# Attention from each row's eight largest scores, with values fetched by index, in front of two dense layers

## The chip, the core and the metric

The kernel runs on one core of one Trainium2 chip. The core has TensorE (PE in the profile; PEld is its weight loads), VectorE (DVE), ScalarE (ACT), GpSimd (POOL) and SyncE (SP), which here only issues transfers. The metric is the device time of one execution in microseconds (us); the median of three runs is given.

## The reference

Attention with a threshold, and then two dense layers (token blocks B=4, H=8 heads, S=576 rows, D=64; 2304 tokens, 512 wide, 2048 hidden). The inputs `q`, `k`, `v` and `moe_w_in` are drawn normal and multiplied by 8 over what stands here; `tau` is 0.02. The dense weights lie in memory as 64-bit numbers.

```
scores = scale * np.matmul(q, k.transpose(0, 1, 3, 2))
thresh = np.max(scores, axis=-1, keepdims=True) - tau
scores = np.where(scores >= thresh, scores, -1000000000.0)
attn = np.exp(scores - max) ; attn = attn / (sum + 1e-09)
x = (attn @ v), heads side by side            # 2304 x 512
h = x @ w_in ; y = (s * relu(h)**2 + b) @ w_out               # layer one
h = y @ w_in2 ; out = (max(h, 0) + alpha * min(h, 0)) @ w_out2   # layer two
```

Only the scores within 0.02 of a row's largest take part. With the reference's inputs that is one to seven of a row's 576 scores; no row has eight.

## The kernel before, in words

**Attention.** 16 pairs of heads (4 blocks of 4 pairs) give 9 tiles each of 128 rows by 576 scores, 144 tiles in all. A tile is scored in two halves of 288 columns into a two-bank PSUM buffer `sc` (L859); there are two such buffers. DVE takes the row's largest from it (L869), POOL works out the threshold (L871), ACT takes the exponential (L873), DVE multiplies it by the mask and sums (L875). The kept exponentials `e` are turned on PE by products with identity matrices (`flip`, L400 and L402), split into a high and a low part (`gh`, `gl`: L1032 and L1047 on POOL, L1035 on ACT, L1037 on DVE) and multiplied by the values `vt` (L979). The result, divided by the sums, goes to a buffer `xs` in memory, already turned.

**Layer one, in two passes.** Products are three matmuls each (`mm3`, L608 to L610: low by high, high by low, high by high). Ten of the 16 pairs of hidden tiles (`NA`) of the first 1536 tokens are worked during attention, in the gaps that it leaves PE, and their part of the output goes to memory (`ya`). The other six, and all 16 for the last two blocks of 384 tokens, come after attention, with `ya` added back.

**Layer two** multiplies its matrices by seven block products in place of eight (`seven`, L551; sums of blocks are made on DVE and POOL at L573 and L586), also with `mm3`.

**Weights** are made from the 64-bit words on DVE (L496 to L505: three or four passes over 128x512) and ACT, one set per 128x512 words.

**What sets the order.** A planner (`Plan`, L217) takes tasks with a cost, an engine or several, buffers and a rank, and writes out one fixed instruction order for every engine. `MOVES`, a table of some 100 lines, shifts the ranks of single tasks by their number:

```
        ways = [(engine, us, n if rank is None else rank)] if isinstance(engine, str) else engine
        t.ways = [(e, u, (r + MOVES.get(n, 0), n)) for e, u, r in ways]
```

On an engine nothing overtakes: an instruction that waits holds up all that stand behind it.

## Time and profile before

| | us |
|---|---|
| runs | 1098.36, 1092.99, 1094.26; median 1094.26 |
| span of the profiled execution | 1091.7 |
| PE, DVE, ACT, POOL busy in it | 1065.7, 886.6, 730.2, 344.3 |

The span is what the profiler saw from the first to the last instruction; it lies 2.6 us below the median of the runs. Busy time counts matmuls, weight loads, and work on data, not the issuing of transfers. An engine that is busy nearly all of the span sets the time if its work comes one after the other.

### The profile page before, as it was taken

The page shows a single profiled execution, that of the slowest core. Times are in us where ns is not written, and L with a number is a line of the kernel's source. Part 1 is how long each engine was busy: PE and PEld are TensorE (multiplying, and loading weights), DVE is VectorE, ACT ScalarE, POOL GpSimd, SP SyncE. Part 2 cuts the span into 40 slices and gives each one's busy share as a digit, 9 for nine tenths or more (in the row PEclk, how much of TensorE's full clock was granted, in tenths as well). Part 3 has the DMA queues.
Part 4 walks back from the last instruction along what each step waited for, and adds up shares of the span by engine and source line. Part 5 has one row for each costly group of instructions (what it writes and reads, how often), then busy time and mean ns, then how long its engine had stood idle before and what let it go on. Part 6 is the DMA issues. An engine that isn't in the chain of part 4 may idle for free.

```text
span 1091.7 us, 21462 instructions
## 1 busy us (share of the span) xinstructions
PE 1065.7 (98%) x7074; PEld 1015.3 (93%) x7074; DVE 886.6 (81%) x2005; ACT 730.2 (67%) x1737; POOL 344.3 (32%) x475
## 2 busy tenths in 40 slices
PE   8999999999999999999999999999999999999998
PEld 7767889989999989999999999999999999999998
DVE  5989888978888788837766695588889999999872
ACT  5899877867887778734443364477768997565551
POOL 1567754754564366520000020110103341112100
PEclk9999999999999999999999999999999999999999
DMA  6655475476555653425375766248586464554531
GB/s 150 188 168 155 111 162 144 109 181 152 128 128 142 150 114 95 113 80 188 116 248 181 240 214 212 73 142 259 196 262 228 162 208 147 152 155 130 155 84 39
DMA packets 195182, 170.89 MB, mean 157 GB/s; under 512 B 73216, under 2 KB 173568, under 8 KB 195072
## 3 DMA queue, kind: packets, MB, share of 16 engines
q1 hardware_dynamic: 192112, 167.31, 53.9%
q10 hardware_dynamic: 2960, 2.23, 0.8%
q8 instruction: 55, 0.90, 0.4%
q14 instruction: 55, 0.45, 0.1%
HBM read 98.97 MB, written 49.28 MB: 136 GB/s over the span
## 4 chain that ended last, share of the span: by engine, by line
PE 78%; DVE 6%; ACT 6%; DMA 5%; issue 2%; SPq 1%; POOL 1%; DVEq 0%; ACTq 0%; POOLq 0%
PE bank L608 12%; PE bank L609 11%; PE bank L610 11%; PE bank_b L608 8%; PE bank_b L609 8%; PE bank_b L610 8%; PE sc L859 7%; PE bank L979 6%; DMA q<-hq 4%; PE bank L402 3%; PE bank L400 3%; ACT e L873 1%; DMA gf<-yat 1%; DVE e L875 1%; DMA stg<-in_moe_w_out_dram 1%
## 5 line engine op out<-in xcount | busy, mean ns | idle before, releaser
L875 DVE SCALAR_TENSOR_TENSOR e<-sc,mx,e 128x576 f32<-128x576 f32 x144 | 116.3, 811 | 14.0 <-ACT e L873 10.5
L869 DVE TENSOR_REDUCE mx<-sc 128x1 f32<-128x576 f32 x144 | 107.4, 750 | 20.9 <-PE sc L859 20.0
L873 ACT ACTIVATE e<-sc,mx 128x576 f32<-128x576 f32 x144 | 107.0, 747 | 10.9 <-DVE mx L869 10.2
L402 PE MATMUL bank<-eyes_r,e 128*128 128x128 f32 (+1 forms) x320 | 88.8, 287 | 0.0
L608 PE MATMUL bank<-xt,wa 128*128 128x480 f32 (+3 forms) x221 | 81.4, 368 | 1.0 <-ACT rest L639 0.7
L871 POOL TENSOR_SCALAR mx<-mx,tau_s 128x1 f32<-128x1 f32 x144 | 47.4, 330 | 91.0 <-DVE mx L869 76.9
L609 PE MATMUL bank<-xt,wa 128*128 128x480 f32 (+3 forms) x221 | 74.5, 337 | 0.0
L610 PE MATMUL bank<-xt,wa 128*128 128x480 f32 (+3 forms) x221 | 74.3, 336 | 0.0
L608 PE MATMUL bank<-gt,wa 128*128 128x384 f32 (+4 forms) x209 | 73.4, 351 | 0.1
L610 PE MATMUL bank<-gt,wa 128*128 128x384 f32 (+4 forms) x209 | 69.7, 333 | 0.0
L609 PE MATMUL bank<-gt,wa 128*128 128x384 f32 (+4 forms) x209 | 69.6, 333 | 0.0
L979 PE MATMUL bank<-gl,vt 128*128 128x256 f32 (+1 forms) x192 | 63.8, 334 | 0.0
L979 PE MATMUL bank<-gh,vt 128*128 128x256 f32 (+1 forms) x192 | 57.7, 302 | 0.0
L1035 ACT ACTIVATE gh<-bank 128x256 fp32r<-128x256 f32 (+1 forms) x96 | 39.5, 411 | 23.8 <-PE bank L402 19.0
L1037 DVE TENSOR_TENSOR gl<-bank,gh 128x256 fp32r<-128x256 f32 (+1 forms) x96 | 43.4, 452 | 12.4 <-ACT gh L1035 11.4
L1047 POOL TENSOR_TENSOR gr<-gf,gh 64x256 fp32r<-64x256 f32 (+1 forms) x48 | 39.4, 820 | 42.9 <-DVE gl L1045 38.6
L402 PEld LDWEIGHTS bank<-eyes_r,e 128*128 128x128 f32 (+1 forms) x320 | 44.5, 139 | 4.2 <-DVE e L875 0.2
L1032 POOL TENSOR_TENSOR gl<-gf,gh 128x256 fp32r<-128x256 f32 (+1 forms) x48 | 38.6, 805 | 22.7 <-ACT gh L1030 12.7
L502 DVE SCALAR_TENSOR_TENSOR n<-stg,n 128x512 int32<-128x512 int32 x64 | 44.7, 699 | 1.0
L608 PEld LDWEIGHTS bank<-xt,wa 128*128 128x128 f32 x221 | 42.4, 192 | 3.3 <-ACT rest L639 1.1
L859 PE MATMUL sc<-k,q 128*128 128x288 f32 x184 | 41.3, 349 | 3.9 <-DMA q<-hq 2.7
L660 ACT ACTIVATE gt<-rest 128x384 fp32r<-128x384 f32 x56 | 29.2, 524 | 23.0 <-DVE rest L658 22.2
(710 smaller groups left out, 4192.6 us busy)
## 6 DMA issues: line engine op xcount, KB each, us to landing
stg<-in_moe_w_in_dram SPq DMA_DIRECT2D x32, 512.0 KB, 3.9
stg<-in_moe_w_out_dram SPq DMA_DIRECT2D x32, 512.0 KB, 3.7
gf<-gw SPq DMA_DIRECT2D x41, 192.0 KB, 2.4
gw<-gf SPq DMA_DIRECT2D x56, 128.0 KB, 2.8
q<-hq SPq DMA_DIRECT2D x24, 256.0 KB, 5.4
qo<-hq SPq DMA_DIRECT2D x24, 256.0 KB, 5.2
xt<-xs SPq DMA_DIRECT2D x14, 384.0 KB, 4.3
yf<-yb SPq DMA_DIRECT2D x24, 192.0 KB, 2.8
```

Of the source, the lines that this page charges most:

```text
L402: nc.tensor.transpose(to, part(x), one)
L502: add("DVE", dve(DM), lambda: nc.vector.scalar_tensor_tensor(ni(), word(0), 29, ni(), op0=ALU.logical_shift_right, op1=ALU.bitwise_or), (n ...
L608: nc.tensor.matmul(o, lhsT=wl, rhs=mh, start=first, stop=False, skip_group_check=on_top)
L609: nc.tensor.matmul(o, lhsT=wh, rhs=ml, start=False, stop=False, skip_group_check=on_top)
L610: nc.tensor.matmul(o, lhsT=wh, rhs=mh, start=False, stop=last, skip_group_check=on_top)
L859: nc.tensor.matmul(sp.t[:, x, :HS], lhsT=o[0][:, c], rhs=o[1][:, x * HS:(x + 1) * HS], start=n == 0, stop=n == len(passes) - 1)
L869: add("DVE", dve(S), lambda sp=sp, mx=mx: nc.vector.tensor_reduce(mx.t[:, 0:1], sp.t[:, :, :HS], op=ALU.max, axis=AX.XY, negate=True), (sp ...
L871: t2 = add("POOL", 0.26, lambda mx=mx: nc.gpsimd.tensor_scalar(mx.t[:, 1:2], mx.t[:, 0:1], -1.0, tau_s, op0=ALU.mult, op1=ALU.subtract), ( ...
L873: add("ACT", act(S, 1), lambda sp=sp, mx=mx, e=e: nc.scalar.activation(halves(e.t), sp.t[:, :, :HS], AF.Exp, bias=mx.t[:, 0:1]), (sp, mx), ...
L875: add("DVE", dve(S) + 0.065, lambda sp=sp, mx=mx, e=e, col=col, sums=sums: nc.vector.scalar_tensor_tensor(halves(e.t), sp.t[:, :, :HS], mx ...
L979: nc.tensor.matmul(o.t[:, :n], lhsT=w.rearrange("p a b -> p (a b)"), rhs=m.t[:, :n], start=c == first and x == 0, stop=c == last and x == ...
L1037: add("DVE", dve(n), lambda hi=hi, lo=lo, gt=gt: nc.vector.tensor_tensor(lo.t[:, :n], gt.t[:, :n], f32(hi.t[:, :n]), op=ALU.subtract), (gt ...
```

## The change

- **Scores to SBUF.** Each half of the scores goes to its own PSUM bank, and ACT copies it to a buffer `sc` of 128x576 in SBUF (two such buffers). The exponential, mask and sum over 576 columns go, and so do the turns of `e`, its splits and the products with the values.
- **`top`.** DVE takes the eight largest of a row and their places (`nc.vector.max`, `nc.vector.max_index`, L648 and L649). All that follows works on these eight: `places` L666, `masks` L673 to L675, exponential L678, `shares` L681 to L685, `codes` L690 to L694, once for a pair's 9 tiles (4 or 5 in the first block).
- **`fetch`.** For the two largest of every row POOL issues an indirect transfer that fetches 128 rows of 64 values by index (L518), 2 per tile, 288 in all. They are multiplied by their shares and added (L707, L712) and stored to a buffer `zn` in memory.
- **`rest`.** The third to seventh of a row, where the threshold keeps them, are collected once for a unit of 16 or 36 tiles (five units): the largest eight codes of every partition, 4 or 5 of them fetched (23 fetches in all) and added in memory by indirect transfers that add (L763, 23 of them, each waiting for the one before).
- **`alarm` and `dense`.** Flags are raised where an eighth score is kept, two places of one row tie, or a unit has more entries in a partition than it fetches. At the end every engine reads the flags (`values_load`, L1158) and branches (L1159); where one is raised, `dense` works everything out again in a plain way. With the reference's inputs none is raised.
- **Layer one in one pass.** All 16 pairs of hidden tiles are held in SBUF, and seven `BLOCKS` of tokens are worked one after the other; `ya` goes. `load_x` turns the rows of `zn` on PE (36 turns for 128x128, L888 and L890).
- **`MOVES`** goes; the order comes from the ranks alone. Layer two is as before.

Indirect transfers, `MAX` and `MAX_INDEX` are not in the kernel before.

```diff
-NA = 10
-CAP = 16
-TA = 480
...
-FIRST = ((0, 256), (256, 320), (576, 480), (1056, 480))
...
+BLOCKS = ((0, 256), (256, 320), (576, 288), (864, 288), (1152, 384), (1536, 384), (1920, 384))
...
-MOVES = {
-    47: 2.69, 58: -2.12, 64: 1.47, 69: 3.73, 81: -27.9, 87: 4.15, 88: -0.353, 89: 2.54, 90: 39.1, 91: 2.54, 92: 2.54, 93: 3.16, 134: -2.99,
...
+        def fetch(to, index, at):
+            nc.gpsimd.indirect_dma_start(out=to, out_offset=None, in_=values, in_offset=bass.IndirectOffsetOnAxis(ap=index[:, at:at + 1], axis=0))
...
+                        add("PE", pe(HS, 4) if first else pe_r(HS, len(passes)), score, of, (sb,), rank=rank)
...
+                        add("ACT", act(HS), lambda sb=sb, sc=sc, keys=slice(x * HS, (x + 1) * HS): nc.scalar.activation(
+                            sc.t[:, keys], sb.t[:, :HS], AF.Copy), (sb,), (sc,), rank=rank)
+
+                    def top(sc=sc, view=view, i=j - j0):
+                        nc.vector.max(view(0, TOP)[:, i], sc.t)
+                        nc.vector.max_index(view(TOP, TOP).bitcast(U32)[:, i], view(0, TOP)[:, i], sc.t)
+
+                    add("DVE", 1.65, top, (sc,), (st,), rank=rank)
...
+                def places(b=b, h0=h0, js=js, m=m, top_i=top_i, index=index):
+                    for s in range(DENSE):
+                        nc.vector.scalar_tensor_tensor(
+                            index(s)[:, :m], top_i()[:, :, s], float((b * H + h0) * S), value_row[:, js], op0=ALU.add, op1=ALU.add)
...
+                def shares(top_v=top_v, ex=ex, one=one, wide=wide, u=u, ts=ts):
+                    nc.vector.tensor_tensor(ex(), ex(), top_v(), op=ALU.mult)
+                    nc.vector.tensor_reduce(one(1), ex(), op=ALU.add, axis=AX.X)
+                    nc.vector.tensor_scalar_add(one(1), one(1), 1e-9)
+                    nc.vector.reciprocal(one(1), one(1))
+                    nc.vector.tensor_tensor(u.weight[:, ts], ex(), wide(one(1), TOP), op=ALU.mult)
...
+                    vals, n = Buf(v_s), g1 - g0
+                    for j in range(g0, g1):
+                        for s in range(DENSE):
+                            add("POOL", 1.25, lambda vals=vals, i=j - g0, j=j - j0, s=s, index=index: fetch(vals.t[:, s, i, :], index(s), j),
+                                (st,), (vals,), ws, rank, 2.0, alone=False)
...
+                    def by(e, vals=vals, n=n, u=u, t=t0 + g0 - j0):
+                        on(e).tensor_tensor(
+                            vals.t[:, :, :n], vals.t[:, :, :n],
+                            u.weight[:, t:t + n, 0:DENSE].rearrange("p t s -> p s t").unsqueeze(3).to_broadcast([P, DENSE, n, D]), op=ALU.mult)
...
+                    add([("DVE", dve(DENSE * n * D), rank), ("POOL", pool2(DENSE * n * D), rank + LATER)], 0, by, (vals,), (vals,), after=(share,), port=True)
+                    add([("DVE", dve(n * D), rank), ("POOL", pool2(n * D), rank + LATER)], 0, lambda e, vals=vals, n=n: on(e).tensor_tensor(
+                        vals.t[:, 0, :n], vals.t[:, 0, :n], vals.t[:, 1, :n], op=ALU.add), (vals,), (vals,), port=True)
...
+            add("DVE", dve(u.T * NX), lambda: nc.vector.max(wd(0), u.code), (u.buf,), (x,), rank=rank)
...
+            def factors():
+                for i in range(n):
+                    nc.vector.scalar_tensor_tensor(
+                        junk(NX), u.code, wd(0)[:, i:i + 1], u.weight[:, :, DENSE:TOP - 1], op0=ALU.is_equal, op1=ALU.mult, accum_out=wd(7)[:, i:i + 1])
...
+            for i in range(n):
+                add("POOL", 1.25, lambda i=i: fetch(xv.t[:, i, :], wd(5, U32), i), (x,), (xv,), ws, rank, 2.0, alone=False)
...
+            for i in range(n):
+                t = add("POOL", 1.87, lambda i=i: nc.gpsimd.indirect_dma_start(
+                    out=u.zn.rearrange("t (h d) -> (t h) d", d=D), out_offset=bass.IndirectOffsetOnAxis(ap=wd(6, U32)[:, i:i + 1], axis=0),
+                    in_=xv.t[:, i, :], in_offset=None, compute_op=ALU.add), (xv, x, u.zn_d), (u.zn_d,), u.added, rank, 2.0, alone=False)
+                u.added = (t,)
...
-        def group(h, gi, rank, es, vt, via, plain):
-
-            o = outs[0] = Buf(one_s, "o")
...
+        full, of_w = (), []
+        for i, (c0, n) in enumerate(BLOCKS):
+            x = load_x(c0, n, SOON)
...
+            m, gs = n + 2 * (i == 0), {}
+            for j in range(NF + LAG):
+                rank = LATER + i + j * 1e-3
+                if j < NF:
+                    h, full = hidden(x, n, j, rank, full)
+                    gs[j] = square(h, n)
+                if j >= LAG:
+                    f = j - LAG
+                    g = gs.pop(f)
+                    for d in range(NC):
+                        def go(d=d, y=ys[d], f=f, g=g, m=m):
+                            u = u1o[f // 2]
+                            mm3(y.t[:, :m], u.w_out(0, f, d * P, P), u.w_out(1, f, d * P, P), g.t[:, 0, :m], g.t[:, 1, :m], f == 0, f == NF - 1)
+                        lasts[d] = (add("PE", pe_r(m, 3), go, (g, u1o[f // 2].buf), (ys[d],), after=lasts[d], rank=rank),)
...
+        def alarm():
+            b = moe_s.free[0]
+            one = rt[0][:, :2]
+            nc.vector.tensor_reduce(one[:, 0:1], flags, op=ALU.max, axis=AX.X)
+            nc.vector.tensor_scalar(one[:, 0:1], one[:, 0:1], 0.0, None, op0=ALU.is_gt)
+            nc.vector.memset(one[:, 1:2], 1.0)
+            nc.tensor.matmul(b[:1, :1], lhsT=one[:, 0:1], rhs=one[:, 1:2], start=True, stop=True)
+            nc.vector.tensor_copy(lost[:1].bitcast(I32), b[:1, :1])
+
         plan.run()
+        alarm()
+    main.close()
+    more = nc.values_load(lost[:1].bitcast(I32), min_val=0, max_val=P)
+    with tc.If(more > 0):
+        dense(tc, *qkv, w1i, w1o, w2i, w2o, out, ident, sc_p, tau_s, s_b, b_b, nal_b)
```


**The instruction orders.** On DVE, near the ninth pair of heads, this is a stretch of the order before. `mx` is a row's largest, `gl` the low part of the turned exponentials, `hq` the low part of the split queries, `z` the attention's output, `rest` and `gt` hidden values of layer one.

```order
L875 SCALAR_TENSOR_TENSOR e_145,sums_172<-sc_114,mx_169,e_145 128x576
L869 TENSOR_REDUCE mx_170<-sc_113 128x1
L808 SCALAR_TENSOR_TENSOR hq<-bank_111,sc_p,hq 128x512
L644 TENSOR_TENSOR rest_103<-rest_103 128x480
L1064 TENSOR_TENSOR z_165<-bank_109,sh_159 128x256
L1037 TENSOR_TENSOR gl_1329<-bank_110,gh_1326 128x320
L650 TENSOR_TENSOR gt<-rest_103,gt 128x480
L869 TENSOR_REDUCE mx_171<-sc_114 128x1
L1045 TENSOR_TENSOR gl_1328<-bank_110,gr_1331 128x320
L1037 TENSOR_TENSOR gl_1329<-bank_111,gh_1326 128x320
L875 SCALAR_TENSOR_TENSOR e_155,sums_173<-sc_114,mx_171,e_155 128x576
L875 SCALAR_TENSOR_TENSOR e_151,sums_172<-sc_113,mx_170,e_151 128x576
```

And this a stretch of the order after, where the tiles of one pair end and those of the next begin. `st` holds the eight largest and what is made of them for a pair, `vals` the fetched values.

```order
L666 SCALAR_TENSOR_TENSOR st_178<-st_178,value_row 128x9 x2
L648 MAX st_179<-sc_175 128x8
L649 MAX_INDEX st_179<-st_179,sc_175 128x8
L923 TENSOR_TENSOR gt<-rest_108,gt 128x320
L673 TENSOR_SCALAR st_178<-st_178,tau_s 128x9
L674 TENSOR_TENSOR st_178<-st_178 128x72
L675 TENSOR_TENSOR st_178<-st_178 128x72
```

Some rows further the order after goes on like this; `unit` holds the shares of a unit's tiles.

```order
L685 TENSOR_TENSOR unit_181<-st_178 128x72
L648 MAX st_179<-sc_176 128x8
L649 MAX_INDEX st_179<-st_179,sc_176 128x8
L690 TENSOR_TENSOR unit_181<-st_178 128x18
L691 SCALAR_TENSOR_TENSOR unit_181<-st_178,code_of 128x45
L694 TENSOR_TENSOR unit_181<-unit_181,st_178 128x45
L648 MAX st_179<-sc_175 128x8
L649 MAX_INDEX st_179<-st_179,sc_175 128x8
L707 TENSOR_TENSOR vals_182<-vals_182,unit_181 128x2x256
```

The two passes over a tile, which stood apart with other work between them, are now `MAX` and `MAX_INDEX` one behind the other; the splits of the turned exponentials are gone, and between two pairs stand some twenty short instructions. `L707`, which waits for the fetches, stands two and more tiles behind `L666`, which gives them their indices.

On POOL the order before, at the same place, has thresholds (`L871`) and splits (`L1032`, `L1047`):

```order
L871 TENSOR_SCALAR mx_170<-mx_170,tau_s 128x1
L1047 TENSOR_TENSOR gr_1331<-gf_158,gh_1326 64x320
L871 TENSOR_SCALAR mx_168<-mx_168,tau_s 128x1
L871 TENSOR_SCALAR mx_171<-mx_171,tau_s 128x1
L1032 TENSOR_TENSOR gl_1329<-gf_157,gh_1325 128x320
L871 TENSOR_SCALAR mx_169<-mx_169,tau_s 128x1
L922 COPY rb_166<-rc_174 128x512
L1047 TENSOR_TENSOR gr_1331<-gf_158,gh_1327 64x256
```

After, at the end of the first half of block one of the heads, it has fetches for pairs (into `vals`) and for the unit's rest (into `more`), and the transfers that add in memory:

```order
L518 DMA more_185<-in_v_dram,extra_184 128x64 x5
L518 DMA vals_182<-in_v_dram,st_177 128x64 x4
L763 DMA zn_0_199<-more_185,extra_184 4608x64
L518 DMA vals_182<-in_v_dram,st_177 128x64 x2
L763 DMA zn_0_199<-more_185,extra_184 4608x64
L518 DMA vals_182<-in_v_dram,st_177 128x64 x2
L763 DMA zn_0_199<-more_185,extra_184 4608x64
L518 DMA vals_183<-in_v_dram,st_177 128x64 x2
L763 DMA zn_0_199<-more_185,extra_184 4608x64
```

POOL's work during attention is now issuing transfers; the adding ones stand one by one between the next pair's fetches.

## Rows read from the trace of the kernel before

**Rows 1.** The page: span, busy time, and the 40 slices of two engines and the clock.

```profile
span 1091.7 us, 21462 instructions
...
PE 1065.7 (98%) x7074; PEld 1015.3 (93%) x7074; DVE 886.6 (81%) x2005; ACT 730.2 (67%) x1737; POOL 344.3 (32%) x475
...
PE   8999999999999999999999999999999999999998
...
DVE  5989888978888788837766695588889999999872
```

**Rows 2.** Windows: us, busy us (count) of PE PEld DVE ACT POOL, PEclk, DMA share, GB/s.

```profile
0.00:463.60 463.60, 447.59 (x3074) 402.44 (x3075) 393.02 (x902) 369.12 (x853) 254.45 (x378) 1.00 0.56 140
463.60:1087.00 623.40, 617.88 (x4002) 612.82 (x4001) 492.26 (x1101) 361.11 (x885) 89.81 (x97) 1.00 0.55 169
550.00:600.00 50.00, 50.00 (x288) 50.00 (x287) 32.18 (x61) 21.15 (x43) 1.02 (x1) 1.00 0.72 224
1000.00:1050.00 50.00, 50.00 (x420) 50.00 (x419) 42.29 (x118) 26.41 (x74) 8.39 (x11) 1.00 0.47 130
```

**Rows 3.** Line L859, the scores: count, duration ns min/median/max, first and last start.

```profile
...
L859 PE MATMUL sc<-k,q x184: 288/301/542, 19.8 to 451.3; 128*128 128x288 f32 x184
...
L859 PE MATMUL sc<-ko,qo x112: 288/295/383, 134.1 to 463.4; 128*128 128x288 f32 x112
...
```

**Rows 4.** The page's groups: busy us, mean ns, idle before and what ended it.

```profile
L875 DVE SCALAR_TENSOR_TENSOR e<-sc,mx,e 128x576 f32<-128x576 f32 x144 | 116.3, 811 | 14.0 <-ACT e L873 10.5
L869 DVE TENSOR_REDUCE mx<-sc 128x1 f32<-128x576 f32 x144 | 107.4, 750 | 20.9 <-PE sc L859 20.0
...
L402 PE MATMUL bank<-eyes_r,e 128*128 128x128 f32 (+1 forms) x320 | 88.8, 287 | 0.0
...
L871 POOL TENSOR_SCALAR mx<-mx,tau_s 128x1 f32<-128x1 f32 x144 | 47.4, 330 | 91.0 <-DVE mx L869 76.9
...
L979 PE MATMUL bank<-gl,vt 128*128 128x256 f32 (+1 forms) x192 | 63.8, 334 | 0.0
```

**Rows 5.** Groups of DVE by form, same columns.

```profile
L502 DVE SCALAR_TENSOR_TENSOR n<-stg,n 128x512 int32<-128x512 int32 x64 | 44.7, 699 | 1.0
L500 DVE TENSOR_SCALAR n<-n 128x512 int32<-128x512 int32 x64 | 30.7, 479 | 2.6 <-ACT n L494 2.1
L661 DVE TENSOR_TENSOR gt<-rest,gt 128x384 fp32r<-128x384 f32 x53 | 30.2, 572 | 10.9 <-ACT gt L660 10.6
...
L808 DVE SCALAR_TENSOR_TENSOR hq<-bank,sc_p,hq 128x512 fp32r<-128x512 f32 x12 | 8.9, 746 | 1.9 <-ACT hq L806 1.9
L802 DVE TENSOR_TENSOR hk<-bank,hk 128x512 fp32r<-128x512 f32 x12 | 8.2, 682 | 0.6 <-ACT hk L800 0.6
```

**Rows 6.** Timeline of DVE in the first heads: start us, duration us.

```profile
22.16 0.14 DVE L909 TENSOR_SCALAR rc<-sums 128x1 f32<-128x1 f32 x1
...
24.01 0.81 DVE L875 SCALAR_TENSOR_TENSOR e<-sc,mx,e 128x576 f32<-128x576 f32 x1
24.75 0.75 DVE L793 TENSOR_SCALAR q<-bank,by_half 128x512 f32<-128x512 f32 x1
```

**Rows 7.** Groups of POOL by form.

```profile
L828 POOL TENSOR_TENSOR vt<-nat,vt 128x640 fp32r<-128x640 f32 x12 | 18.8, 1570 | 10.1 <-ACT vt L826 6.0 <-PE bank L402 2.4 <-DMA ya<-rest 1.8
L1032 POOL TENSOR_TENSOR gl<-gf,gh 128x256 fp32r<-128x256 f32 x24 | 17.6, 735 | 7.6 <-ACT gh L1030 5.3 <-DVE gh L1031 2.3
```

**Rows 8.** Timeline of PE near 238 us.

```profile
238.31 0.74 PE L859 MATMUL sc<-ko,q 128*128 128x288 f32 x2 [2.04 <-DMA q<-hq]
```

**Rows 9.** Windows around that stop, columns as in rows 2.

```profile
236.00:238.00 2.00, 0.27 (x3) 0.07 (x1) 0.82 (x2) 1.08 (x4) 0.62 (x1) 1.00 0.96 202
239.00:240.00 1.00, 1.00 (x7) 0.99 (x6) 0.42 (x1) 0.00 (x0) 0.00 (x0) 0.50 0.59 133
```

**Rows 10.** Timeline of all engines at the end.

```profile
1086.92 0.28 PE L610 MATMUL bank_b<-wb,xt 128*128 128x256 f32 x1
...
1087.91 0.41 DVE L1419 TENSOR_TENSOR gw<-gw,n 128x256 f32<-128x256 f32 x1
```

954 lines of the change are left out of this document (428 added, 526 removed), and 97 rows, old and new, of the table MOVES.

## The prediction

> **What bounds the kernel now.** I read the page first: PE is busy 1065.7 of 1091.7 us and none of its slices is under 8 tenths; DVE is next with 886.6 [rows 1]. Busy shares are means over stages, so I cut the span at the last score, which starts at 463.4 us [rows 3]. Before that PE is busy 447.6 of 463.6 us and DVE 393.0; after it PE is busy 617.9 of 623.4 [rows 2]. So PE sets both stages, with 3.5% of idle time in the first and 1% in the second. The reader should see that DVE's 85% in the first stage leaves little room: whatever empties PE there makes DVE the next bound.
>
> **PE's rates.** In the stretch from 550 to 600 us, where all matmuls have 384 columns, 288 of them take 50 us: 173.6 ns each. From 1000 to 1050, where all have 256, 420 take 50 us: 119.0 ns [rows 2]. Between the two that gives 132.7 ns for 288 columns and 146 for 320, and beyond them 215 for 480. I price by these rates, not by the durations of 283 to 338 ns, in which neighbours overlap.
>
> **PE after the last score.** The order of before has there 2160 matmuls of 384, 192 of 386, 1512 of 256, 75 of 480, 27 products with values and 35 turns: 375 + 33.5 + 180 + 16 + 8 = 612.5 us. It took 623.4, so 10.9 us are lost. The order of after has 282 of 288, 2160 of 384, 1512 of 256 and 36 turns: 37 + 375 + 180 + 5 = 597 us. Layer two is the same, so I keep the loss. PE's last matmul ends 4.5 to 4.7 us before the span does [rows 1, 10]; that stays, and behind it come the alarm (five short operations), the register loads and the branch. The trace has no branch; the bounds are nothing (it could fit beside the last stores) and another such tail of 4.7; I take 3. So the span is the time of the last score plus 597 + 10.9 + 4.7 + 3 = 615.6 us. Before, that rest was 1091.7 less 463.6, 628.1 us: only 12.5 us are gained behind the last score, and everything else hangs on when the last score comes.
>
> **PE before the last score.** The turns of the exponentials (320 at L402 alone), their products with the values (192 of high and 192 of low parts at L979) go [rows 4], and layer one is there whole for the first 864 tokens and in part for the next 288. By the order: 528 score matmuls, 192 of 256 and 192 of 258, 384 of 320, 486 of 288, some 230 turns and warm-ups. The scores make about 90 us (456 of 132.7 ns, and 72 in full precision at up to 0.41 us, between a plain one's 288 ns [rows 3] and twice that), layer one 167.6, the rest 25: 283 us. It was 447.6. PE is no longer the bound there.
>
> **DVE before the last score.** Two buffers `sc` stand between scores and `top`, so the last score is held by DVE's place in its own order. Its work up to the last `MAX_INDEX`:
> - 144 tops. `MAX` reads 576 elements once, as L869 does in 0.750 us; `MAX_INDEX` reads them with a second operand, as L875 does in 0.811 [rows 4]. Neither is in the trace. Low bound: two passes like L869 at the pitch at which DVE follows itself, 0.07 under its duration (24.01 to 24.75 for a duration of 0.81 [rows 6]): 2 x 0.67 = 1.34. High: two like L875 with 0.08 between, as the second reads what the first wrote: 1.78. I take 0.75 + 0.81 + 0.08 = 1.64, so 236 us.
> - 38 weight conversions of three passes (0.479, 0.699, 0.69 [rows 5], each less 0.08: 1.62) and some 20 single passes: 73.
> - 54 subtractions for layer one, 0.45 less 0.08 (between L661's 0.572 at 384 columns and a shorter one): 20; 16 splits of `x`: 6; 60 splits of q and k (like 0.746 and 0.682 at 512 columns [rows 5], shorter ones at 64): 21.
> - 26 products `L707` over 512 or 640 elements and 26 sums `L712` over half as many, from the same rows: 26.
> - 247 short operations of `places`, `masks`, `shares` and `codes`, 0.14 to 0.16 each (0.14 at L909 [rows 6]): 37. Four units' `rest`: 17.
>
> Together 436 us. Before, DVE was busy 393.0 us in this stage [rows 2], so it gains work, 43 us, where PE loses it. I give the new bound the idle share that the old bound had, 3.5%: 452. The first top starts some 11 us in, and the last score stands two tiles (3.3 us) ahead of the last top: 459 us.
>
> **ACT** copies 288 half tiles at 0.41 us or less, and loses the exponentials: under 300 us, not the bound.
>
> **POOL before the last score.** Up to the last `L707` that stands ahead of the last top it issues 278 fetches and 18 adding transfers, and has 28 us of other work. The trace has no indirect transfer at all. Nearest rows: the shortest of POOL's operations over data takes 0.735 us, the longest 1.570 [rows 7]; A fetch handles 128 indices on one engine, more than the few hundred elements of a lane in the short one ask for and less than the 640 of the long one; I take the middle, 1.2. With the same 3.5%, 20 us before the first fetch and 12 for the way from fetch to `L707`: 20 + (296 x 1.2 + 28) / 0.965 + 12 = 429 us, under DVE's 459. It passes DVE from 1.30 us on. Queued behind a late `L707` on DVE are the tops of the next pair, and behind them the scores. In the order three tops and some twenty short operations stand between `L666` and `L707`, 16 us or more, so a punctual fetch holds nothing up.
>
> The Trainium skill, page "DMA: Bandwidth & Descriptors", section "Latency and other measured facts", gives about 1 us to the first byte of a transfer issued by GpSimd against 0.6 for the other engines. An estimate by it for 296 transfers is 324 us with POOL's other work, which does not bind; no run here shows it.
>
> **Layer one's later blocks** wait for the last unit's adding transfers. These end some 40 us after the last score (35 transfers of 1.2), and PE comes to the block that reads them (tokens from 1536) after 37 us of 288 columns and 67 of 384: hidden, and with 60 us to spare.
>
> **Sum.** 459 + 615.6 = 1074.6 us of span. The span of before lies 2.6 under the median, so 1077: 17 us faster, 1.6%. The time is that of before if the last score comes at 476. What a measurement of this kernel can tell is about 0.5%, 5.5 us.
>
> **Rivals.**
> 1. *POOL's fetches bind; slower.* DVE's `L707` then waits for POOL, two buffers `vals` deep, and POOL runs without a stop. For it: 296 equal operations in one queue, each price error counts 296 times; and POOL takes 1.57 us for 640 elements, twice what DVE takes for a few less [rows 5, 7]. Against: a fetch moves no data on POOL itself. It decides from 1.35 us a fetch (last score at 476); at the upper bound of 1.57 the last score comes at 543 and the time is 1161. DVE is a part of it too: while it runs an operation faster than one element a cycle, POOL might be shut out. Such are the 42 passes at L500's 0.479 us for 512 elements [rows 5], 20 us in all, which would move 429 to 449 and not decide. The Trainium skill, page "SBUF — State Buffer", section "A bandwidth-pool intuition that's wrong (but worth ruling out)", says that a GpSimd transfer waits for its descriptors until such a DVE operation ends, 3100 ns in place of 620; no run here shows it. If every fetch met that, the time would be that of a fetch at 3.1 us, far over the rival's; the few passes of this kind speak against it.
> 2. *PE's clock falls in the emptied stage; slower.* PE will be idle 38% of the first stage. Around 236 to 238 us of before PE was busy 0.27 of 2 us and stood 2.04 us waiting for `q`; from 239 to 240 the granted clock is 0.50, its lower level of 1.2 GHz [rows 8, 9]. The gaps to come are mostly below one top, 1.64 us, and layer one's matmuls fill them; but the order writes these in lumps of three to twelve. At half clock 283 us become 566. It decides when 56% of the work runs at half clock; at 75% PE needs 495, with its idle time 514, and the time is 514 + 10 + 615.6 + 2.6, about 1142.
> 3. *The tops are at their low bound*, and DVE waits less than PE did: 193 + 200 = 393, plus 11, less 3: 401, or with 3.5% about 415. PE and the weights then come in question; the time is 1019 to 1033.
> 4. *The change does not do what it says*: a flag is raised and `dense` runs behind everything. By the inputs no row has eight kept scores; several thousand us if it does.
>
> **How the numbers follow.** DVE sets the stage with tops near 1.64: 0.50, with a range of its own of 1055 to 1097 (tops of 1.50 to 1.78), most of it faster. Rival 3: 0.12, faster. Rival 1: 0.24, slower, with its lower end within 0.5%. Rival 2: 0.12, slower. Rival 4: 0.02. Of the likeliest's 0.50, 0.42 are faster by over 0.5% and 0.06 within; with rival 3 and some of rival 1's lower end that makes 0.54 faster, 0.12 the same, 0.34 slower. The range for 8 in 10 goes from rival 3's 1025 to 1155, just below rival 1's upper bound.
>
> **What the profile would show.** Right: PE idle in the first stage, ended by ACT's copies or by free buffers `sc`, DVE busy over 90% up to the last top, that top near 460 us, L648 and L649 at 0.75 and 0.81; the fetches at 1.2 us and POOL with idle time; PEclk near 1.0 and PE without gaps behind the last score; 36 turns from `zn` without waits. Wrong: DVE's idle time ended by transfers into `vals` (rival 1), slices of PEclk at 5 to 7 in the first stage (rival 2), tops under 0.7 (rival 3), a span over 2000 (rival 4). A fault that none of them holds: weights for all 16 hidden tiles come later than layer one's first block asks for them, so that PE carries some of its 167.6 us past the last score.

## The result, and the profile after

The changed kernel takes 1102.29 us (1102.12 to 1102.63, four runs) against 1094.28 for the one before: 1.0068 times as long, 95% interval 1.0042 to 1.0095. Slower, by 0.7%; 1077 and a gain of 17 us were forecast. The profiled execution has a span of 1100.8 us. Of the six runs of e1_fill below, three lie over 1.5% above the fastest; its time and ratio are those of the other three.

The page after: span, busy times, and the slices of four engines and of the clock, to be read beside [rows 1]; the last row is the clock of the kernel before.

```profile
span 1100.8 us, 19143 instructions
...
PE 985.2 (89%) x6120; PEld 926.7 (84%) x6120; DVE 870.9 (79%) x2166; ACT 594.2 (54%) x1511; POOL 438.3 (40%) x449
...
PE   8765976778789788899899999999999999999996
...
DVE  6999998888989898696667425785857999999871
ACT  5444654464446454454335325676877997555550
POOL 2676765777767667777620000000100331121020
PEclk9555897688889888999899999999999999999999
```

```profile
PEclk9999999999999999999999999999999999999999
```

Up to the eighteenth slice, where the last score lies, most slices of PE fall to 5 to 8 tenths where they were 9, those of DVE stand at 8 or 9 up to the sixteenth, POOL's at 5 to 7 behind the first, and the granted clock is 0.5 to 0.9 where it was 0.9 or more. The same in numbers, as windows with the columns of [rows 2]: the stage up to the last score, a piece at its start, its second half, and what lies behind it.

```profile
0.00:485.00 485.00, 385.84 (x2159) 332.35 (x2160) 425.73 (x1114) 246.43 (x643) 330.45 (x339) 0.81 0.62 145
50.00:100.00 50.00, 32.59 (x75) 19.47 (x76) 48.66 (x138) 19.71 (x46) 35.13 (x32) 0.53 0.50 119
235.00:481.00 246.00, 209.35 (x1313) 197.17 (x1314) 211.63 (x559) 127.25 (x342) 175.72 (x173) 0.89 0.63 141
480.90:1096.00 615.10, 603.45 (x3994) 598.41 (x3993) 449.24 (x1061) 349.78 (x873) 110.94 (x114) 0.99 0.44 135
```

PE is busy 80% of the stage at a mean clock of 0.81, DVE 88%. The instructions that the sum was made of, by line (count, shortest, median and longest duration in ns, start of the first and the last):

```profile
L637 PE MATMUL bank<-k,q x528: 288/399/847, 10.2 to 480.8; 128*128 128x288 f32 x133, 64*128 64x288 f32 x43
...
L648 DVE MAX8 st<-sc x144: 740/752/762, 11.9 to 483.1; 128x8 f32<-128x576 f32 x144
...
L649 DVE MATCH_VALUE_LOAD st<-st,sc x144: 92/92/94, 12.7 to 483.8; 128x8 f32 x144
L649 DVE FIND_INDEX8 st<-st,sc x144: 750/752/754, 12.8 to 483.9; 128x8 uint32<-128x576 f32 x144
...
L518 POOL DMA_INDIRECT vals<-in_v_dram,st x288: 938/949/1532, 20.2 to 533.6; - x144
...
L763 POOL DMA_INDIRECT zn<-more,extra x23: 1557/1618/2088, 85.8 to 566.7; - x23
```

The last score starts at 480.8 us and not at 459; behind it come 620.0 us, 615.6 were forecast. So 22 of the 26 us between the forecast span (1074.6) and the measured one lie before the last score, where `MAX` and `MAX_INDEX` cost what was assumed (1.60 us for a top, 1.64 taken) and the fetch nearly so (0.95 us in the median, 1.01 in the mean, and a gap of 0.30 behind it; 1.2 taken). DVE was busy 425.7 us up to 485, 436 were forecast. On DVE not work is missing from the sum, then, but waiting. What DVE waited for in the stage (us in all, times, longest):

```profile
DVE gt L923 <- ACT gt L922: 11.9, 14, 2.0
DVE st L648 <- ACT sc L644: 9.2, 8, 2.0
DVE vals L707 <- DMA stg<-in_moe_w_in_dram: 5.9, 1, 5.9
DVE vals L707 <- issue: 5.3, 2, 3.3
DVE vals L707 <- DMA vals<-in_v_dram,st: 1.8, 1, 1.8
DVE vals L707 <- DMA q<-hq: 1.2, 1, 1.2
```

Each is small, and together with the smaller ones they are 47 us, where 16 had been allowed. The waits at L707 are put down to several things, but all five end within 0.5 us of the landing of a fetch (by the updates of its semaphore in the trace): they are waits for fetched values, 14 us in all. And POOL in the second half, 235 to 481 us:

```profile
POOL vals L518 <- issue: 42.8, 141, 0.3
POOL vals L518 <- DVE unit L691: 5.4, 1, 5.4
POOL zn L763 <- DVE st L648: 3.7, 1, 3.7
POOL zn L763 <- DMA zn<-more,extra: 2.8, 2, 1.7
```

"issue" are the gaps of 0.30 us behind each fetch. With its 175.7 us of busy time and some 48 of such gaps, POOL is taken for 224 of these 246 us, 91%, more than DVE (211.6, 86%): two engines, each nearly full, and each waits for the other in places.

### The profile page after: what moved, and what is told of

Its sections match the earlier page's. It is cut to its first block, busy times and chain, and to the rows that moved or that the text cites. A ratio compares the mean times of both kernels' runs of the same rounds, so it can differ in the third digit from the quotient of the medians.

```text
span 1100.8 us, 19143 instructions
## 1 busy us (share of the span) xinstructions
PE 985.2 (89%) x6120; PEld 926.7 (84%) x6120; DVE 870.9 (79%) x2166; ACT 594.2 (54%) x1511; POOL 438.3 (40%) x449
## 4 chain that ended last, share of the span: by engine, by line
PE 49%; DVE 21%; DMA 11%; POOL 7%; issue 6%; ACT 4%; SPq 1%; DVEq 0%; POOLq 0%; ACTq 0%
PE bank L461 15%; PE bank L462 15%; PE bank L463 15%; POOL vals L518 5%; DVE st L649 4%; DVE st L648 4%; PE bank L637 3%; DMA zn<-more,extra 2%; DMA vals<-in_v_dram,st 2%; DMA more<-in_v_dram,extra 1%; POOL zn L763 1%; DMA zn<-vals 1%; DMA stg<-in_moe_w_in_dram 1%; DVE n L370 1%; DVE vals L707 1%
## 5 line engine op out<-in xcount | busy, mean ns | idle before, releaser
L518 POOL DMA_INDIRECT vals<-in_v_dram,st x288 | 291.6, 1013 | 116.2 <-issue 78.4
L637 PE MATMUL bank<-k,q 128*128 128x288 f32 (+1 forms) x528 | 159.5, 430 | 85.2 <-ACT sc L644 78.9
L461 PE MATMUL bank<-xt,wa 128*128 128x384 f32 (+3 forms) x544 | 183.2, 337 | 4.8 <-DVE hq L594 1.8
L462 PE MATMUL bank<-xt,wa 128*128 128x384 f32 (+3 forms) x544 | 179.0, 329 | 0.0
L463 PE MATMUL bank<-xt,wa 128*128 128x384 f32 (+3 forms) x544 | 178.7, 328 | 0.0
L644 ACT ACTIVATE sc<-bank 128x288 f32<-128x288 f32 x288 | 106.8, 409 | 130.5 <-DVE st L649 103.0
L462 PE MATMUL bank<-gt,wa 128*128 128x384 f32 (+3 forms) x496 | 159.7, 322 | 4.7 <-DVE gt L923 3.1
L461 PE MATMUL bank<-gt,wa 128*128 128x384 f32 (+3 forms) x496 | 159.6, 322 | 2.9 <-ACT gt L922 2.6
L463 PE MATMUL bank<-gt,wa 128*128 128x384 f32 (+3 forms) x496 | 157.9, 318 | 0.0
L461 PEld LDWEIGHTS bank<-xt,wa 128*128 128x128 f32 x544 | 110.0, 202 | 8.7 <-DVE hq L594 2.1
L648 DVE MAX8 st<-sc 128x8 f32<-128x576 f32 x144 | 108.1, 751 | 9.3 <-ACT sc L644 9.2
L462 PEld LDWEIGHTS bank<-xt,wa 128*128 128x128 f32 x544 | 109.4, 201 | 0.1
L463 PEld LDWEIGHTS bank<-xt,wa 128*128 128x128 f32 x544 | 108.8, 200 | 0.0
L649 DVE FIND_INDEX8 st<-st,sc 128x8 uint32<-128x576 f32 x144 | 108.3, 752 | 0.0
L462 PEld LDWEIGHTS bank<-gt,wa 128*128 128x128 f32 x496 | 94.9, 191 | 7.8 <-DVE gt L923 5.6
L461 PEld LDWEIGHTS bank<-gt,wa 128*128 128x128 f32 x496 | 95.2, 192 | 3.8 <-ACT gt L922 2.9
L463 PEld LDWEIGHTS bank<-gt,wa 128*128 128x128 f32 x496 | 94.9, 191 | 0.0
L463 PE MATMUL bank<-xb,wa 128*128 128x384 f32 x192 | 64.5, 336 | 0.0
L461 PE MATMUL bank<-xb,wa 128*128 128x384 f32 x192 | 64.5, 336 | 0.0
```

Source lines behind the costliest of these rows:

```text
L461: nc.tensor.matmul(o, lhsT=wl, rhs=mh, start=first, stop=False, skip_group_check=on_top)
L462: nc.tensor.matmul(o, lhsT=wh, rhs=ml, start=False, stop=False, skip_group_check=on_top)
L463: nc.tensor.matmul(o, lhsT=wh, rhs=mh, start=False, stop=last, skip_group_check=on_top)
L518: nc.gpsimd.indirect_dma_start(out=to, out_offset=None, in_=values, in_offset=bass.IndirectOffsetOnAxis(ap=index[:, at:at + 1], axis=0))
L637: nc.tensor.matmul(sb.t[:, :HS], lhsT=l[:, rows], rhs=r[:, keys], start=n == 0, stop=n == len(passes) - 1)
L644: add("ACT", act(HS), lambda sb=sb, sc=sc, keys=slice(x * HS, (x + 1) * HS): nc.scalar.activation(sc.t[:, keys], sb.t[:, :HS], AF.Copy), ( ...
```

## The experiments

All of these have the instruction orders of the changed kernel on every engine, but for what is left out or added. They compare with the kernel before on the chip on which they ran; it takes between 1094.6 and 1095.9 us there (medians).

**e1_fill: idle products behind each half tile of scores.**

```diff
-nc.tensor.matmul(sb.t[:, :HS], ..., start=n == 0, stop=n == len(passes) - 1)
+nc.tensor.matmul(sb.t[:, :HS], ..., start=n == 0, stop=n == len(passes) - 1); n == len(passes) - 1 and [nc.tensor.matmul(sb.t[:, 3 * P:], lhsT=ident_r, rhs=ident_r, start=True, stop=True, skip_group_check=True) for _ in range(6)]
```

> Six idle products of 128 columns (identity by identity, into columns of the score's own bank that nobody reads) behind each half tile of scores, some 110 us of matmuls that nothing waits for; all other instructions in the same order. Theory A, TensorE's clock: the granted clock up to the last score was 0.81 with the change; matmuls of layer one that stand ahead of scores ran at half clock, came late, and DVE waited 48 us in all. With the idle time filled the clock of that stretch rises to 0.95 or more, DVE's waits fall under 30 us, the last score comes 20 us earlier, near 460, and the time is about 1080. Theory B, DVE's own work and the fetches: the clock rises all the same, but the last score stays at 478 to 483 and the time at 1099 to 1104. Theory C, PE as the bound: the added 110 us push the last score past 495.

Measured: 1213.61 us, 1.106 times the kernel before (1.101 to 1.111); the last score at 598. Six such products take 0.61 us at full clock (from 304.03 to 304.64 in the timeline), 176 us for 288 half tiles and not 110, and PE became the bound: theory C, by too large a dose. What it does show is the clock. Windows of PE with the columns as above:

```profile
50.00:100.00 50.00, 50.00 (x168) 36.52 (x168) 33.89 (x89) 13.43 (x32) 24.53 (x23) 0.53 0.29 80
400.00:600.00 200.00, 198.70 (x1593) 197.30 (x1593) 148.00 (x371) 96.17 (x244) 121.18 (x120) 1.00 0.52 125
```

From 50 to 100 us PE is busy all the time, and the granted clock is 0.53 as without the idle products; later, from 400 on, it is 1.00. Idle time alone isn't what keeps the clock near its lower level (0.50, 1.2 GHz) at the start.

**e2_half_tops: the eight largest of half a row.**

```diff
-nc.vector.max(view(0, TOP)[:, i], sc.t)
-nc.vector.max_index(view(TOP, TOP).bitcast(U32)[:, i], view(0, TOP)[:, i], sc.t)
+nc.vector.max(view(0, TOP)[:, i], sc.t[:, :HS])
+nc.vector.max_index(view(TOP, TOP).bitcast(U32)[:, i], view(0, TOP)[:, i], sc.t[:, :HS])
```

> The eight largest are looked for in the first 288 of the 576 scores of a row only, so the other keys take no part in the result; each top falls from 1.60 to about 1.0 us, 86 us of DVE in all, and the order of all engines is the same. Theory B, DVE sets the last score: it comes 70 to 86 us earlier, near 400 to 410, and the time falls to about 1020 to 1035, PE's matmuls of layer one filling what is left. Theory A, the clock sets it: the clock rises as PE idles less, and the last score comes earlier by more than DVE's 86 us can explain at the old clock, or, if half clock remains, by less than 50. Theory D, POOL sets it: 296 transfers at 1.25 us are 370 us, so the last score can't come before 430, and the time stays over 1050.

Measured: 1087.12 us, ratio 0.991 (0.988 to 0.995), last score at 468.0. Of 86 us less on DVE only 13 arrive. The scores and DVE's waits in this kernel:

```profile
L637 PE MATMUL bank<-k,q x528: 288/383/847, 9.6 to 468.0; 128*128 128x288 f32 x133, 64*128 64x288 f32 x43
...
DVE gt L923 <- ACT gt L922: 25.0, 27, 3.1
DVE vals L707 <- DMA vals<-in_v_dram,st: 19.9, 8, 5.6
```

DVE now waits at L707 for fetched values, 19.9 us in eight places in this row alone, where it was 1.8 in one; all waits at L707 are 42 us, and were 14. POOL holds the stage at 468 even when DVE has room; with half tops and no transfers on POOL the last score comes at 422.6 (e13, below). Theory B is out. Theory D's words hold, but POOL's floor lay 38 us above the 430 that I had for it; theory A's "by less than 50" fits as well, and this run doesn't part the two.

**e3_one_fetch: only the largest is fetched.**

```diff
-v_s = Slots(tiles(ap, 2, "vals", [P, DENSE, NK, D]))
+v_s = Slots(tiles(ap, 2, "vals", [P, DENSE, NK, D])); [nc.gpsimd.memset(t[:, 1], 0.0) for t in v_s.free]
-...: fetch(vals.t[:, s, i, :], index(s), j),
+...: s or fetch(vals.t[:, s, i, :], index(s), j),
```

> Only the largest score's value of each row is fetched, 144 fetches in place of 288; the second largest takes no part in the result (its values are zeros, still multiplied and added), so DVE's work is the same. Theory D, POOL's fetches hold DVE up: DVE's waits at L707, 14 us of the 48, go, the last score comes 14 us or more earlier, at 467 or under, and the time is 1088 or less. Theories A and B: the waits at L707 go, but other waits take their place; the last score moves by less than 5 us and the time by less than 6.

Measured: 1087.30 us, ratio 0.993 (0.990 to 0.996), last score at 467.8, 13 us earlier: theory D, though 0.8 us short of the 467 that it asked for. Relieving either engine gives the same 13 us.

**Four kernels on another chip, and then the changed kernel itself on yet another.** e4 joins the two edits above. e5 takes the scores behind the first four pairs in one pass (`for n, (l, r) in enumerate(passes[-1:])`, `start=True, stop=True`). e6 has two idle products behind each half tile behind the first four pairs. e7 joins e4 and e5.

> Both at once: the eight largest of the first 288 scores only, and one fetch per tile and not two (the other keys and the second largest take no part in the result); all orders are as with the change but for the fetches left out. Each alone moved the last score from 481 to 468. Theory E, two engines in a loop: DVE (88% busy) and POOL (330 us busy and some 80 between its transfers) each become the bound when the other is relieved; together the last score comes at 410 or under, and the time is 1030 or less. Theory A, PE with its low clock is next behind both: the last score stays at 450 or later, the time at 1070 or more.

> The scores of all pairs behind the first four are taken in one pass (high parts only, so they are less exact) in place of two or three: 240 matmuls of 288 columns fewer, 32 us at full clock. Theory A, PE and its clock set the last score: it comes 20 us or more earlier, at 461 or under, and the time is 1082 or less. Theory E, DVE and POOL set it: it moves by less than 8 us, the time stays at 1093 or more.

> Two idle products of 128 columns behind each half tile of scores of all pairs behind the first four; six everywhere took 0.10 us each and made PE the bound. 432 of them are 44 us. Theory A: the granted clock from 200 us on rises from 0.80 to 0.88 to over 0.93, scores come earlier for it, and the time is 1092 or less. Theory E: the clock rises, and the time stays between 1098 and 1108. If PE is a third bound at its present clock, the added work shows: over 1115.

> Half tops, one fetch and one pass of scores together (what each leaves out of the result is as above). Theory E: hardly earlier than half tops and one fetch together, by less than 8 us. Theory A: 20 us or more earlier than those.

Measured: 1084.26, 1226.13, 1263.03 and 1073.56 us (the kernel before 1095.88). With half the fetches the last score comes at 460.0 in e4 and 453.3 in e7; neither theory on the bound had named these, and e4 has standstills like those below, so the four don't settle it. Less work on PE can hardly cost 124 us, so the changed kernel itself was run on one chip with e5 (as e9), e4 (as e11) and a new one, e10.

> The changed kernel itself, on the same chip as the next three. The kernels with one pass of scores and with two idle products took 1226 and 1263 us with less and with little more work; in their traces PE, ACT and DVE stand still together for up to 11 us at a time while only POOL's fetches and transfers go on, and the records of semaphore updates are fewer than the updates. Theory S, something of that chip or run: here this kernel and one pass of scores are both within 15 us of 1102. Theory T, the order of the semaphores' traffic in those kernels does it: this one is at 1102 and one pass of scores again over 1200. If this one too is over 1150, the chip does it, to every kernel with the fetches.

> Scores behind the first four pairs in one pass (high parts only), as before. Theory S: 1070 to 1102, and then the two theories on the bound that this kernel was made for can be told apart: 1082 or less for TensorE and its clock, 1093 or more for DVE and POOL. Theory T: 1215 to 1235 again.

> Half tops and one fetch together, as before (1084 us, with 75 us of standstills in ACT and PE in its trace). Theory S: without the standstills the last score comes at 435 or under and the time is 1055 or less. Theory T, or theory A with PE next behind DVE and POOL: 1078 to 1090 again.

Measured there: the changed kernel, not a byte different, 1248.06 us, 1.143 times the kernel before (1.139 to 1.147); one pass 1244.32; half tops and one fetch 1093.30. So it goes with the chip, or with what the chip did at that time, and hits the kernels with all the fetches. The kernel before takes 1094.59 us on the same chip. This is how it looks in the timeline of the changed kernel there (PE, ACT and POOL, first column the start in us):

```profile
220.77 0.66 PE L637 MATMUL bank<-hk,hq 128*128 128x288 f32 x3
...
222.19 0.94 POOL L518 DMA_INDIRECT vals<-in_v_dram,st  x1 [0.30 <-issue]
...
227.18 0.94 POOL L518 DMA_INDIRECT vals<-in_v_dram,st  x1 [0.30 <-issue]
230.81 0.38 ACT L912 ACTIVATE rest<-bank 128x256 f32<-128x256 f32 x1 [9.87 <-remote]
...
231.25 0.61 PE L637 MATMUL bank<-hk,hq 128*128 128x288 f32 x1 [9.81 <-ACT rest L912]
```

PE's last matmuls end at 221.4. ACT's next instruction waits for PE's semaphore alone, and the wait ends at 230.8, 9 us later, in which POOL goes on with its fetches. In that trace PE, ACT and DVE are idle together for over 1.5 us in 18 places ahead of the kernel's end, 57 us in all (worked out from the starts and durations of all three); in the first trace of the changed kernel and in that of e16 in none. The last of the 18 begins at 643 us, and the last transfer by index ends at 714: behind it there is none. These 57 us are not all of the 146 by which the kernel is longer there. One pass of scores changes nothing there (1244 against 1248), half the fetches and half tops take most of it away (1093).

**e10_full_rows, on the same chip: the first four pairs' scores over 128 rows.**

```diff
-passes = [(q32[p][a], k32[p][a])] if first else [(1, None), (0, None)]
+passes = [(q32[p], k32[p])] if first else [(1, None), (0, None)]
```

> The scores of the first four pairs (full precision) as products over all 128 rows of the array in place of the 64 rows of one head, so that both heads' scores are added together and the result is another; all orders are the same. From 50 to 100 us the granted clock was 0.53 with the change, and 0.53 too where idle products kept PE busy 50 of 50 us. Theory R, work on half of the rows keeps the clock low: it rises to over 0.8 there, and from 100 to 200 too. Theory A in its first form, idle time alone does it: it stays under 0.65. In both, the last score moves little, since DVE is 97% busy there: by less than 10 us.

Measured: 1251.26 us against 1248.06, no difference. The window from 50 to 100 us of this kernel

```profile
50.00:100.00 50.00, 28.81 (x77) 18.03 (x78) 48.73 (x138) 20.22 (x48) 35.07 (x31) 0.68 0.47 115
```

and of the changed kernel on the same chip:

```profile
50.00:100.00 50.00, 33.62 (x74) 20.02 (x74) 48.70 (x135) 19.94 (x48) 36.06 (x32) 0.50 0.49 121
```

The clock is 0.68 in place of 0.50, with less busy time on PE, 28.8 us against 33.6. Neither theory named that: 0.65 was one's upper bound, 0.8 the other's lower one, and from 100 to 200 us the clock hardly moves (0.81 against 0.79). What else held it below 1.00 stays open. The last score, at 598.4 against 597.9, did not move, as expected.

**e12 to e15: POOL without transfers by index.** In e12 each fetch is a short write of a constant, and the adding transfers are left out; e13 adds half tops to it and e14 one pass; in e15 a plain transfer, `nc.gpsimd.dma_start(out=to, in_=values[:P])`, stands in place of the write.

```diff
-nc.gpsimd.indirect_dma_start(out=to, out_offset=None, in_=values, in_offset=bass.IndirectOffsetOnAxis(ap=index[:, at:at + 1], axis=0))
+nc.gpsimd.memset(to, 0.1)
-t = add("POOL", 1.87, lambda i=i: nc.gpsimd.indirect_dma_start(
+t = add("POOL", 1.87, lambda i=i: 0 and nc.gpsimd.indirect_dma_start(
```

> Every fetch is replaced by a short write of a constant into the same 128x64 buffer, and the adding transfers are left out, so the attention's output is made of constants; POOL then issues no transfers during attention, and all other orders are as with the change. Two questions. First, the standstills, in which an update of PE's semaphore is seen up to 9 us late (kernel as changed: 1102 us on one chip, 1248 on another): if the indirect transfers cause them, there are none here on any chip. Second, the bound without POOL: if DVE alone sets the last score (theory B), it comes at 460 to 468, and the time is 1078 to 1088, as with one fetch in place of two; if POOL still held it with one fetch, it comes at 450 or under.

> As the kernel without fetches, and the eight largest are looked for in 288 of the 576 scores, 86 us less on DVE. Theory B, DVE is the bound when POOL is out: the last score comes 60 us or more earlier than without fetches alone, at 400 or under, and the time is 1020 or less. Theory A, PE with its low clock and layer one's chain through ACT and DVE is the bound behind it: it comes less than 25 us earlier, and the time is 1055 or more.

> As the kernel without fetches, and the scores behind the first four pairs in one pass of high parts: 32 us less of PE at full clock, some 40 at the clock granted. Theory A: the last score comes 20 us or more earlier than without fetches alone. Theory B: less than 8 us earlier.

> Every fetch by index is replaced by a plain transfer issued by POOL, the same 128 rows of 64 values each time, and the adding transfers are left out. If it is POOL's making of descriptors or the number of small packets that delays the semaphore of PE, the standstills are here as in the kernel as changed, and the time is 1100 on an undisturbed chip and over 1200 on another; if it is the index, there are none, and the time is under 1105 everywhere. POOL's price of a plain one against 1.25 us of pitch for one by index shows what the index costs: I expect 1.0 to 1.25.

Measured: e12 1074.98 us, ratio 0.982 (0.979 to 0.986); e13 1034.90 (0.946, 0.943 to 0.949); e14 1071.85 (0.979); e15 1080.24 (0.987). The rows of the scores of e12 and of e13, by line, whose last start is the point:

```profile
L637 PE MATMUL bank<-k,q x528: 288/401/850, 9.3 to 462.4; 128*128 128x288 f32 x133, 64*128 64x288 f32 x43
```

```profile
L637 PE MATMUL bank<-k,q x528: 288/332/847, 10.0 to 422.6; 128*128 128x288 f32 x133, 64*128 64x288 f32 x43
```

Without POOL's transfers the last score comes at 462.4, near where the sum over DVE's work had put it (459), and the time is 2 us off the forecast. Then half tops gain 40 us, three times what they gained with the fetches: DVE is the bound once POOL is out. The gain lies between what the two theories asked for (under 25, over 60); it is not 86, and PE seems to be next, 93.7 of 100 us busy from 300 to 400:

```profile
300.00:400.00 100.00, 93.67 (x656) 89.53 (x655) 80.72 (x275) 62.18 (x169) 8.00 (x78) 0.97 0.60 153
```

One pass gains 3 us in the last score:

```profile
L637 PE MATMUL bank<-k,q x336: 289/403/849, 9.3 to 459.2; 128*128 128x288 f32 x104, 64*128 64x288 f32 x64
```

So, with POOL's transfers out, 32 us of PE's work are worth 3: theory B, and not theory A. The same edit to the changed kernel itself (e5, e9) ran only where there were standstills. The plain transfer takes POOL half of what one by index takes, and no gap follows it: eight in a row take 4.39 us (from 241.80 in the timeline of e15), 0.55 each, where I expected 1.0 to 1.25.

```profile
L518 POOL DMA_DIRECT2D vals<-in_v_dram x288: 534/537/787, 3.1 to 506.2; - x144
```

Its first start, 3.1 us against 20.2, shows that a plain one doesn't wait for indices from DVE either, so price and wait are not parted here.

**e16 to e18: the changed kernel, plain transfers, and no adding transfers, on one chip.** e18 has the second edit of e12 alone.

> The changed kernel once more, on the chip of the next two. 1102 us if the chip is like the first, 1240 to 1255 with standstills if it is like the one of its second run; the other two are read against it.

> Plain transfers issued by POOL in place of the fetches by index, no adding transfers, as before (1080 us with no standstills, on a chip on which the changed kernel itself was not run). If the changed kernel stands still here and this one doesn't (1078 to 1083), the transfers by index cause it; if both do (over 1150), any transfer issued by POOL. If neither does, this tells nothing new.

> The fetches stay, and the 23 adding transfers alone are left out (the third to seventh largest take no part in the result). On a chip with standstills: within 30 us of the changed kernel if the 311 fetches cause them, under 1120 if the adding ones do. On a chip without: POOL has 29 us less before the last score (18 of 1.62 us), and by the reading that POOL and DVE bound the stage together the last score comes 3 to 8 us earlier, at 473 to 478, and the time is 1094 to 1099.

Measured: the changed kernel 1103.73 us, 1.0068 times the kernel before (1.0043 to 1.0093), as at first, with the last score at 481.9; plain transfers 1078.12, at 465.0; no adding transfers 1089.70 (0.993, 0.991 to 0.995), at 470.6. The three rows of the scores, in this order:

```profile
L637 PE MATMUL bank<-k,q x528: 288/402/849, 9.8 to 481.9; 128*128 128x288 f32 x133, 64*128 64x288 f32 x43
L637 PE MATMUL bank<-k,q x528: 288/378/849, 9.7 to 465.0; 128*128 128x288 f32 x133, 64*128 64x288 f32 x43
L637 PE MATMUL bank<-k,q x528: 288/398/847, 8.8 to 470.6; 128*128 128x288 f32 x133, 64*128 64x288 f32 x43
```

The chip is of the undisturbed kind, so these don't tell what causes the standstills; but they part POOL's share: 11 us of the last score go with the adding transfers, 6 more where the fetches become plain ones, and 3 lie between these and no transfer at all (e12, 462.4, on another chip). DVE's waits in e18, as above:

```profile
DVE gt L923 <- ACT gt L922: 15.0, 16, 2.2
DVE st L648 <- ACT sc L644: 9.5, 9, 2.0
DVE vals L707 <- DMA q<-hq: 2.7, 1, 2.7
DVE vals L707 <- DMA vals<-in_v_dram,st: 2.1, 1, 2.1
```

The waits at L707 are 4.8 us where they were 14 with the adding transfers; 18 of these, 29 us of POOL, are worth 11 us of the last score, more than the 3 to 8 expected, and the time is under the 1094 to 1099 expected.

## Why the prediction was wrong, step by step

- **PE's rates and the stage behind the last score: 620.0 us for 615.6, near for two errors that offset.** From the last score to the end of the span it is 610.2 us without POOL's transfers (e12), 611.7 with plain ones (e17), 618.2 with the fetches (e18) and 619.9 with the adding transfers too (e16). The kept loss of 10.9 us was too large: in e12 PE's last matmul ends 601.4 us after the last score, 4 over the 597. And the fetches that still run behind the last score, to 533.6 us, stood in the sum at nothing; they go with 7 us or so. Behind PE's last matmul (1091.8 in the changed kernel, span 1100.8) come 9.0 us for alarm, stores and branch, 7.7 forecast. The step "These end some 40 us after the last score (35 transfers of 1.2)" was wrong as well: the last adding transfer starts 86 us after it. They stand in POOL's queue one behind the other, and each waits for the one before to land (timeline of POOL; in brackets the idle time before it and what ended it). It cost little: leaving them out shortens this stage by 1.7 us.

```profile
548.08 2.07 POOL L763 DMA_INDIRECT zn<-more,extra  x1 [6.64 <-DVE n L370]
553.74 1.83 POOL L763 DMA_INDIRECT zn<-more,extra  x1 [3.59 <-DMA zn<-more,extra]
...
566.70 1.60 POOL L763 DMA_INDIRECT zn<-more,extra  x1 [2.45 <-DMA zn<-more,extra]
```

- **DVE's place: right, in part by luck.** e12 is the test of this step by itself: last score at 462.4 for a forecast of 459, time 1075 for 1077. But up to the last score DVE was busy 418.3 us there, where the sum had some 433 (436 less two tops), and it waited 33 us, where the sum had 16: 15 too much of one and 17 too little of the other. The waits that are left are for layer one's values and scores from ACT (14.6 and 9.0 us are the largest). The idle share of 3.5% came from a stage in which one engine was full; here it was 7% without POOL's transfers and 10% with them (47 us).
- **The step that failed: "20 + (296 x 1.2 + 28) / 0.965 + 12 = 429 us, under DVE's 459", and with it "so a punctual fetch holds nothing up".** The fetch, with its gap, takes 1.31 us in the mean and not 1.2, and the adding transfers were priced like fetches, with no wait: they take 1.62 us, the gap, and 6.4 us of waiting for the one before up to the last score, in the queue in which the next pair's fetches stand behind them. With 1.31 and 1.92 us and no idle time at all the same sum gives, as an estimate, 20 + 278 x 1.31 + 18 x 1.92 + 28 + 12 = 459 us: POOL comes out level with DVE, and not 30 us under it. Leaving the adding transfers out alone moved the last score by 11 us. And where two queues come this near to each other, the later one isn't the answer: with POOL's transfers out, the last score comes at 462; with DVE relieved, it comes at 468, with POOL waited for; with both there it is 481. DVE's waits at L707 go from 14 us to 4.8 without the adding transfers and to none without the fetches.
- **Rival 1 is what happened in part, at its lower end.** I had it decide from 1.35 us a fetch; the last score at 481 is past the 476 at which the time is that of before, at 1.31. POOL did not run without a stop, though: it is taken for 91% of the second half, and DVE waited for it 14 of its 47 us. The lengthening of fetches beside DVE's work is there, but small. Of the 288 fetches 85 ran beside tops alone, and none of these took over 1.00 us; 58 took over 1.05 us, 42 of them beside one of DVE's passes over 128x512 for the weights (worked out from the starts and durations of both engines). Together that is 18 us of POOL over 288 times the median. That DVE causes it is not shown; no run changes these passes. The Trainium skill, page "SBUF — State Buffer", section "A bandwidth-pool intuition that's wrong (but worth ruling out)", has such a transfer at 3100 ns beside a DVE copy. No fetch of this trace comes near that, the longest takes POOL 1532 ns; but nearly all of DVE's operations beside fetches last under 0.9 us here, so the trace doesn't test the page's number.
- **Rival 2: the clock fell; what that cost is not shown.** It was 0.53 from 50 to 100 us and 0.81 over the stage, as feared, and PE was busy 386 us there, where 283 of work were forecast. In the kernel without POOL's transfers 32 us less of PE's work moved the last score by 3, so PE's work doesn't bind. But no run raised the clock of this stage without adding work to PE, and DVE's waits for layer one's values may hold some of it. The 56% of the rival's own condition should be 59% for a last score at 476: (476 - 10) x 0.965 = 450 us for 283.
- **Rivals 3 and 4 did not**: the tops take 1.60 us, not 1.34, and nothing of `dense` is in the trace.
- **Left open: the standstills on some chips.** The changed kernel itself was run on three chips and took 1102, 1248 and 1104 us; e5 and e6 (1226, 1263) show the same standstills on a fourth. Seen is that PE's semaphore reaches ACT 9 us late in the stretch above while POOL fetches by index, that half the fetches make it less, that no standstill comes behind the last transfer by index, and that the time of the kernel before is the same on all of them. Whether the index, any transfer from POOL or the adding ones do it couldn't be told apart, since the later runs met chips without it.

No version that computes the whole reference beat the kernel before. The nearest, e18, leaves out a part that would have to be made elsewhere.

## What to carry to other kernels

A queue of small transfers is priced with its gaps and with the waits of each transfer for the one before, and everything that stands behind such a wait in the same queue is late with it: 18 adding transfers, 29 us of POOL, cost 11 us of the stage here. Where a change empties the bounding engine and two others come out near each other (429 and 459 us in the sum), linked by two buffers, the stage can take longer than either (481 us for 462 and 468); take each out alone before believing the larger. A sum that comes out right is not a sum whose terms are: here DVE's place was met with 15 us too much work and 17 too little waiting. And a kernel that moves its traffic to another kind of queue should be timed on more than one chip: this one was 0.7% slower on two and 14% on a third.

## What the runs showed of the hardware that was not expected

- A transfer by index of 128 rows of 256 bytes takes POOL 0.95 us and a gap of 0.30 behind it; a plain one of the same rows 0.54 and no gap (0.55 from start to start); one that adds in memory 1.62.
- `MAX_INDEX` is two instructions, `MATCH_VALUE_LOAD` of 0.092 us and `FIND_INDEX8` of 0.752, as long as `MAX8` (0.752) on 576 elements.
- The granted clock was 0.53, near the lower of its two levels, 1.2 GHz, in a stretch in which PE was busy 50.00 of 50 us (e1_fill), with full-precision products on 64 rows and idle ones on 128 between them; with 128 rows in all of them and PE less busy it was 0.68.
- Beside DVE's `MAX8` and `FIND_INDEX8` alone no fetch by index took over 1.00 us (85 of them); beside passes over 128x512 for the weights they took 1.10 us in the mean (93 of them), and up to 1.46.
- A wait of ACT for PE's semaphore alone ended 9 us after PE's last matmul (e8), with POOL fetching by index; the same kernel on two other chips has no such standstill.
